# Loading q and k in 1 KB runs, with a fixed order of Pool and SP work, in a fused attention and mixer kernel

## The chip, the cores and the metric

The kernel runs on one core of a Trainium2 chip. The metric is the device time of one execution in microseconds (us). A run gives the median of several executions, and one execution is recorded by the hardware profiler. Executions of one kernel agree within 1.2% here (1.7% in e3, one of whose runs counts as slow). Comparisons use executions that ran on the same chip in the same rounds.

The engines are called PE (TensorE, matmuls), PEld (its weight loads), DVE or Vector, ACT or Scalar, POOL or Pool (GpSimd), and SP (SyncE, which here only issues transfers).

## The reference

There are 8 batches of 576 tokens with 8 heads of 64. Attention is limited to a window of 32 tokens on each side, plus 8 global tokens that see all and are seen by all. The result, 576 x 512 per batch, goes through a token mixer and a channel mixer:

```python
scores = scale * np.matmul(q, k.transpose(0, 1, 3, 2))       # q, k, v: (8, 8, 576, 64) float32
mask = (np.abs(pos[:, None] - pos[None, :]) <= 32) | is_global[:, None] | is_global[None, :]
attn = softmax(np.where(mask, scores, -1e9)); attn_out = np.matmul(attn, v)
x = attn_out.transpose(0, 2, 1, 3).reshape(8, 576, 512)
h = np.maximum(x^T @ w_tok1, 0.0) @ w_tok2;  u = x + h^T     # token mixer, 576 -> 256 -> 576
out = u + np.maximum(u @ w_ch1, 0.0) @ w_ch2                 # channel mixer, 512 -> 1536 -> 512
```

## The kernel before

The kernel is software-pipelined. While the channel mixer of batch b ("dense") keeps PE busy, the attention and token mixer of batch b+1 ("sparse") are threaded between its matmuls. Only batch 0 has nothing to hide behind, so the time has two parts: a **start**, up to the first channel matmul, and a **steady part**, from there to the end. A scheduler decides the order of the instructions on each engine when the kernel is built.

The parts that the change and the argument touch:

```python
# the list of global indices, to every partition: 8 low words out of 8 int64
nc.scalar.dma_start(out=gidx_b, in_=bass.AP(tensor=gt32, offset=0, ap=[[0, P], [2, NG]]))
# batch 0: q and k through SP in runs of 256 B (one token of one head)
    nc.sync.dma_start(out=n32[ti][:, 0 : NT - 1, h, :],
                      in_=ten[0, h, 0 : S - LAST, :].rearrange("(t p) d -> p t d", p=P))
# batches 1 to 7: Pool issues DMAs that cast float32 to float16 on the way
def load(b): ...
    nc.gpsimd.dma_start(out=dst[b % 2][0:n, t], in_=ten[b, :, P * t : P * t + n, :].rearrange("h p d -> p h d"))

def T(b, p):                                   # one pair of heads: ten transposes, two copies
    pT = pss([P, 2, 8 * P], F16, name=f"pT_{b}_{p}")
    for ti, n in enumerate((qn, kn)):
        for t in range(NT):                    # NT = 5, the last tile has 64 tokens and 64 rows of zeros
            nc.tensor.transpose(out=pT[:, ti, P * t : P * t + P], in_=n[b % 2][:, t, 2 * p : 2 * p + 2, :], identity=ident)
    nc.vector.tensor_copy(out=qTs[b % 2][:, p, :, GW:QS], in_=pT[:, 0, 0 : NT * P].rearrange("p (t x) -> p t x", t=NT))
    nc.vector.tensor_copy(out=kTs[b % 2][:, p, WIN:], in_=pT[:, 1, 0 : NT * P])

# S_(b, p): scores, exponentials on Scalar into e_all, then on Vector the product eg and for each head a mask:
        nc.vector.tensor_mul(out=eh, in0=eh, in1=bandm)            # 128 x 1040, float16
# PV(b, tau): values; the product with the global rows comes first, over 128 rows
            nc.tensor.matmul(ps[:, hf, 0 : NP * VW], lhsT=s["lf"][:, P * tau - sh : P * tau - sh + P],
                             rhs=s["rf"][:, 2 * hf : 2 * hf + 2], start=True, stop=False)
# M2: token mixer's second product, u = x + ...; M3: transposing DMA u -> uT; M4: first channel product from uT (b1p)
# gather(t): indirect DMAs that fetch the global rows of q and k (t = 0: batches 0-3, t = 1: batches 4-7)
```

The softmax here doesn't subtract the row's maximum and nothing guards it: scores larger than these inputs give would overflow.

Of the kernel before, what the change touches and what calls it, by code (L numbers as in the profile page):

```python
# [8 lines left out]
F32 = mybir.dt.float32  # L9
# [6 lines left out]
P = 128  # L16
# [26 lines left out]
def kernel(  # L43
# [30 lines left out]

    def pss(shape, dtype=F32, name="s"):
        return psS.tile(shape, dtype, tag="s", name=name)
# [8 lines left out]
    n32 = [mb.tile([P, NT, H, D], F32, tag="b1", bufs=1, name="n32_q")]  # L85
    n32 += [const.tile([P, NT, H, D], F32, name=f"n32_{n}") for n in "kv"]
# [15 lines left out]
    for ti, ten in enumerate((q, k)):  # L102
        nc.sync.dma_start(
            out=n32[ti][0:LAST, NT - 1], in_=ten[0, :, S - LAST : S, :].rearrange("h p d -> p h d")
        )
    for p in range(NP):
        for ti, ten in enumerate((q, k)):
            for h in (2 * p, 2 * p + 1):
                nc.sync.dma_start(
                    out=n32[ti][:, 0 : NT - 1, h, :],  # L110
                    in_=ten[0, h, 0 : S - LAST, :].rearrange("(t p) d -> p t d", p=P),
                )
    for c in range(NT):
        r0, r1, j0 = vrows(c)
        nc.sync.dma_start(
            out=n32[2][r0:r1, c], in_=v[0, :, j0 : j0 + (r1 - r0), :].rearrange("h p d -> p h d")
        )

    def load(b):
        for t in range(NT):  # L120
            n = P if t < NT - 1 else LAST
            for ten, dst in ((q, qn), (k, kn)):
                nc.gpsimd.dma_start(  # L123
                    out=dst[b % 2][0:n, t], in_=ten[b, :, P * t : P * t + n, :].rearrange("h p d -> p h d")
                )
        for c in range(NT):
            r0, r1, j0 = vrows(c)
            nc.gpsimd.dma_start(  # L128
                out=vsh[b % 2][r0:r1, c, :, 0:D],
                in_=v[b, :, j0 : j0 + (r1 - r0), :].rearrange("h p d -> p h d"),  # L130
            )

# [10 lines left out]
    make_identity(nc, ident)  # L143

# [30 lines left out]

    gather(0)


    for i in range(2):
        nc.vector.memset(qn[i][LAST:P, NT - 1], 0.0)  # L180
        nc.vector.memset(kn[i][LAST:P, NT - 1], 0.0)
        nc.vector.memset(vsh[i][0:WIN, 0], 0.0)
        nc.vector.memset(vsh[i][P - WIN : P, NT - 1], 0.0)
        nc.vector.memset(vsh[i][:, :, :, D + 1 : VW], 0.0)
        nc.vector.memset(vsh[i][:, :, :, D : D + 1], 1.0)
    e_all = const.tile([P, H, NT, EW], F16)
    nc.vector.memset(e_all[:, :, :, 0:64], 0.0)
    nc.vector.memset(e_all[:, :, 0, 64:P], 0.0)
    nc.vector.memset(e_all[:, :, NT - 1, 64 + GW + P :], 0.0)
    eg = const.tile([P, NT, H, GW], F16)  # L190
    qTs = [const.tile([P, NP, NT, QS], F16, name=f"qT{i}") for i in range(2)]
    kTs = [const.tile([P, NP, WIN + NT * P], F16, name=f"kT{i}") for i in range(2)]
    x16s = [const.tile([P, NT, DM], F16, name=f"x16_{i}") for i in range(2)]
    for i in range(2):
        nc.vector.memset(qTs[i][:, :, :, NG:GW], 0.0)
        nc.vector.memset(kTs[i][:, :, 0:WIN], 0.0)
    nc.vector.memset(kgz, 0.0)
    nc.vector.memset(x16s[0][LAST:P, NT - 1, :], 0.0)
    nc.vector.memset(x16s[1][0:LAST, NT - 1, :], 0.0)
# [7 lines left out]
    nc.vector.memset(w1l, 0.0)  # L207
    nc.vector.memset(w2[:, :, S:], 0.0)
# [3 lines left out]
    nc.gpsimd.dma_start(out=w2[:, :, 0:S], in_=moe_w_tok2.rearrange("(c p) x -> p c x", p=P))  # L212

# [11 lines left out]


    pm16 = int_op("pm16", 15, ALU.bitwise_and)
    p16 = int_op("p16", 4, ALU.logical_shift_right)
# [43 lines left out]

    band = const.tile([P, 192], F16)
    nc.gpsimd.memset(band, 1.0)
    left, right = band[:, 0:64], band[:, 64:192]
    nc.gpsimd.affine_select(out=left, in_=left, compare_op=ALU.is_ge, fill=0.0, base=0, pattern=[[1, 64]], channel_multiplier=-1)
    nc.gpsimd.affine_select(out=right, in_=right, compare_op=ALU.is_ge, fill=0.0, base=64, pattern=[[1, P]], channel_multiplier=-1)
    nc.gpsimd.affine_select(out=right, in_=right, compare_op=ALU.is_ge, fill=0.0, base=0, pattern=[[-1, P]], channel_multiplier=1)
# [14 lines left out]
    it_i = const.tile([P, NT * P], I32)  # L293
    nc.gpsimd.iota(it_i, pattern=[[1, NT * P]], base=0, channel_multiplier=0)
    mf = const.tile([P, NT * P], F16)
    it_f = const.tile([P, NT * P], F32)
# [5 lines left out]
    cc_i = const.tile([P, H], I32)  # L302
    nc.gpsimd.iota(cc_i, pattern=[[1, H]], base=0, channel_multiplier=0)
    blk = const.tile([P, H], F32)
    nc.vector.tensor_copy(out=blk, in_=cc_i)
    nc.vector.tensor_scalar(out=blk, in0=blk, scalar1=p16, scalar2=None, op0=ALU.is_equal)
# [16 lines left out]
    def cast0(p):  # L323

        for ti, dst in enumerate((qn, kn)):
            for t0, n, r in ((0, NT - 1, P), (NT - 1, 1, LAST)):
                hs = slice(2 * p, 2 * p + 2)
                (nc.scalar.copy if ti == 0 else nc.vector.tensor_copy)(  # L328
                    out=dst[0][0:r, t0 : t0 + n, hs], in_=n32[ti][0:r, t0 : t0 + n, hs]
                )  # L330
# [297 lines left out]
```

## Time and profile before

| before | value | from |
|---|---|---|
| time, median of 3 runs | 393.42 us (393.25 to 395.27) | runs |
| first scores | 44.6 us | timeline |
| first value product | 61.2 us | timeline |
| first channel matmul (end of the start) | 87.35 us | timeline |
| from there to the end of the span | 304.6 us | timeline |

The page gives the engines' busy time over the whole span:

```profile
PE 319.8 (82%) x2697; PEld 167.3 (43%) x2697; DVE 185.6 (47%) x400; ACT 137.2 (35%) x269; POOL 114.7 (29%) x156
```

That average mixes two regimes. In the steady part PE is the limit. The windows view (columns: window, its length, then busy us and instruction count of PE, PEld, DVE, ACT and POOL, the granted PE clock, DMA share, GB/s) shows a score stage of a later batch of the kernel before:

```profile
172.00:176.00 4.00, 4.00 (x40) 1.85 (x39) 3.15 (x8) 3.74 (x8) 1.68 (x2) 1.00 0.01 1
176.00:180.00 4.00, 3.71 (x49) 1.43 (x45) 3.05 (x7) 4.00 (x11) 4.00 (x6) 1.00 1.91 123
180.00:184.00 4.00, 4.00 (x42) 2.05 (x33) 3.00 (x6) 2.47 (x6) 3.73 (x6) 1.00 2.32 148
```

PE is full. But DVE stands at 3 us of every 4 there, and its results feed PE, so it has little room. (Pool is "busy" with issuing the casting DMAs, 873 ns each for q on the page.)

The places where PE waited in the steady part, from the waits view (total us, times, longest):

```profile
PE b1p_0_3083 L509 <- DMA uT_3004<-u_5_2972: 1.3, 1, 1.3
PE b1p_0_1117 L509 <- DMA uT_1038<-u_1_1006: 0.8, 1, 0.8
```

At the first channel matmul of each odd batch PE waits 0.7 to 2.0 us (0.79, 0.68, 1.30 and 2.00 in the timeline) for the transposing DMA (SP line 498), which turns u into uT.

Three groups of instructions of the page matter later (busy us, mean ns of one, idle time before and its releaser): the masks, the product eg, and the first scores.

```profile
L390 DVE TENSOR_TENSOR e_all<-e_all,bandm 128x1040 f16<-128x1040 f16 x64 | 42.4, 704 | 0.5
L384 DVE TENSOR_TENSOR eg<-e_all,bandm 128x160 f16<-128x160 f16 x32 | 7.7, 242 | 31.0 <-ACT e_all L383 31.0
L364 PE MATMUL s_0_0_288<-qT_168,kT_170 64*128 64x208 f16 x4 | 0.5, 357 | 14.5 <-POOL qT_168 L339 14.5
```

Finally the start. The DMA view of the first 16 us (first line: GB/s in 40 slices of 0.4 us; then a queue; then issues with KB each and median us to landing):

```profile
GB/s 0 0 0 0 0 0 5 61 152 111 0 0 0 0 0 0 0 0 0 0 0 0 0 0 0 0 0 0 0 0 0 12 38 52 76 94 109 156 176 214
q10 hardware_dynamic: 1184, 0.00, 3.3%
n_q<-in_q_dram SPq DMA_DIRECT2D x3, 128.0 KB, 16.0
gidx_b<-in_global_idx_dram ACTq DMA_DIRECT2D x1, 4.0 KB, 14.4
```

From 4 to 12.4 us the core moves next to nothing, with q and k already issued. A 4 KB index list takes 14.4 us to land.

### The profile page before, as it was taken

What the parts mean: (1) busy time and instruction counts of PE and PEld (TensorE: products, weight loads), DVE (VectorE), ACT (ScalarE), POOL (GpSimd) and SP (SyncE); (2) the same over time, 40 slices, a digit from 0 to 9 for tenths busy, and PEclk for the clock granted to TensorE, in tenths of its full rate; (3) what the DMA queues carried; (4) which work ended last, traced back from release to release, by engine and by line L of the source; (5) the groups of instructions that cost most, each with busy time, mean ns of one, the idle gap of its engine ahead of it and who ended that gap; (6) DMA issues with size and microseconds to landing.
All of it is one profiled execution on the core that took longest, in us unless ns stands there. A gap on an engine that the chain in (4) does not pass through costs nothing.

```text
span 391.9 us, 6622 instructions
## 1 busy us (share of the span) xinstructions
PE 319.8 (82%) x2697; PEld 167.3 (43%) x2697; DVE 185.6 (47%) x400; ACT 137.2 (35%) x269; POOL 114.7 (29%) x156
## 2 busy tenths in 40 slices
PE   0010255659999999999999999999899999997995
PEld 0010234324454465444544654455446545453552
DVE  5342254344645563566445635664456356644012
ACT  2001250106710861077118610761086107710610
POOL 4520798922820372028203720282000000000000
PEclk9999999688999999999999999999999999999999
DMA  0799999991985398419853984298600041005012
GB/s 14 122 198 206 182 141 94 122 114 8 125 79 147 21 115 75 136 30 129 79 147 22 117 75 135 35 126 81 145 0 2 28 136 28 2 28 149 0 55 80
DMA packets 143071, 34.56 MB, mean 88 GB/s; under 512 B 134336, under 2 KB 138304, under 8 KB 143040
## 3 DMA queue, kind: packets, MB, share of 16 engines
q0 software_dynamic: 102832, 16.42, 56.1%
q1 hardware_dynamic: 33776, 8.26, 11.2%
q10 hardware_dynamic: 6432, 9.44, 7.2%
q8 instruction: 21, 0.34, 0.4%
q14 instruction: 10, 0.08, 0.1%
HBM read 36.11 MB, written 9.44 MB: 116 GB/s over the span
## 4 chain that ended last, share of the span: by engine, by line
PE 59%; ACT 9%; DMA 3%; DVE 1%; SPq 1%; issue 1%; ACTq 0%
ACT e_all L374 2%; ACT e_all L383 2%; ACT e_all L382 1%; ACT e_all L381 1%; SPq L498 1%; DMA out_dram<-osb_0_2979 1%; DMA uT_3972<-u_7_3940 1%; PE op_4_4213 L535 1%; PE op_2_3013 L535 1%; PE op_2_2030 L535 1%; PE op_2_1047 L535 1%; PE op_2_3981 L535 1%; PE op_0_2938 L535 1%; PE op_0_3463 L535 1%; PE op_3_4197 L535 1%
## 5 line engine op out<-in xcount | busy, mean ns | idle before, releaser
L509 PEld LDWEIGHTS <-wc_184 128*128 128x128 f16 x384 | 33.0, 98 | 45.1 <-issue 15.8
L390 DVE TENSOR_TENSOR e_all<-e_all,bandm 128x1040 f16<-128x1040 f16 x64 | 42.4, 704 | 0.5
L123 POOL DMA_DIRECT2D qn_80<-in_q_dram x20 | 17.5, 873 | 60.6 <-PE pT_3_1738 L347 22.8
L439 PEld LDWEIGHTS <-e_all 128*128 128x128 f16 x320 | 25.2, 101 | 2.1 <-issue 1.0
L123 POOL DMA_DIRECT2D qn_79<-in_q_dram x15 | 13.2, 883 | 40.2 <-PE pT_3_1217 L347 20.1
L384 DVE TENSOR_TENSOR eg<-e_all,bandm 128x160 f16<-128x160 f16 x32 | 7.7, 242 | 31.0 <-ACT e_all L383 31.0
L128 POOL DMA_DIRECT2D vsh_84<-in_v_dram x20 | 16.9, 865 | 14.4 <-PE pv_2_916 L444 1.5
L347 PE MATMUL pT_0_266<-ident,qn_79 128*128 128x128 f16 x5 | 0.7, 309 | 23.1 <-ACT qn_79 L328 23.1
L444 PEld LDWEIGHTS <-e_all 128*128 128x128 f16 x256 | 19.0, 101 | 1.3
L347 PEld LDWEIGHTS <-qn_79 128*128 128x128 f16 x80 | 6.1, 106 | 28.4 <-ACT qn_79 L328 23.1
L364 PEld LDWEIGHTS <-kT_170 64*128 64x128 f16 x160 | 6.2, 103 | 27.4 <-issue 13.8
L123 POOL DMA_DIRECT2D kn_82<-in_k_dram x20 | 17.6, 878 | 0.0
L128 POOL DMA_DIRECT2D vsh_83<-in_v_dram x15 | 12.7, 881 | 9.6 <-PE b1lp_0_1385 L522 1.1
L328 ACT CAST qn_79<-n_q 64x128 f16<-64x128 f32 (+1 forms) x8 | 3.4, 456 | 32.8 <-DMA n_q<-in_q_dram 32.8
L481 PEld LDWEIGHTS <-w_183 128*128 128x128 f16 x80 | 8.2, 103 | 12.6 <-issue 4.8
L123 POOL DMA_DIRECT2D kn_81<-in_k_dram x15 | 13.3, 888 | 0.0
L364 PE MATMUL s_0_0_288<-qT_168,kT_170 64*128 64x208 f16 x4 | 0.5, 357 | 14.5 <-POOL qT_168 L339 14.5
L336 POOL CAST vsh_83<-n_v 32x512 f16<-32x512 f32 (+1 forms) x9 | 6.2, 697 | 19.3 <-DMA n_v<-in_v_dram 19.1
L522 PEld LDWEIGHTS <-wc_184 128*128 128x128 f16 x192 | 11.1, 98 | 0.6
L364 PEld LDWEIGHTS <-kT_171 64*128 64x128 f16 x160 | 5.2, 95 | 12.8 <-issue 8.5
L463 PEld LDWEIGHTS <-w_181 128*128 128x128 f16 x64 | 6.3, 101 | 6.4 <-issue 1.9
L539 DVE TENSOR_TENSOR osb_0_4162<-u_7_3940,op_0_4149 128x512 f32<-128x512 f16 x1 | 0.7, 689 | 17.1 <-PE op_0_4149 L535 17.1
(1059 smaller groups left out, 821.1 us busy)
## 6 DMA issues: line engine op xcount, KB each, us to landing
qn_80<-in_q_dram POOLq DMA_DIRECT2D x16, 128.0 KB, 4.6
kn_82<-in_k_dram POOLq DMA_DIRECT2D x16, 128.0 KB, 4.6
wc_184<-in_moe_w_ch_dram POOLq DMA_DIRECT2D x3, 512.0 KB, 10.3
wc_185<-in_moe_w_ch_dram POOLq DMA_DIRECT2D x3, 512.0 KB, 8.0
vsh_84<-in_v_dram POOLq DMA_DIRECT2D x12, 128.0 KB, 3.5
qn_79<-in_q_dram POOLq DMA_DIRECT2D x12, 128.0 KB, 4.2
kn_81<-in_k_dram POOLq DMA_DIRECT2D x12, 128.0 KB, 4.2
n_q<-in_q_dram SPq DMA_DIRECT2D x9, 128.0 KB, 7.6
```

The source lines that it names most:

```text
L123: nc.gpsimd.dma_start(out=dst[b % 2][0:n, t], in_=ten[b, :, P * t : P * t + n, :].rearrange("h p d -> p h d"))
L128: nc.gpsimd.dma_start(out=vsh[b % 2][r0:r1, c, :, 0:D], in_=v[b, :, j0 : j0 + (r1 - r0), :].rearrange("h p d -> p h d"),)
L364: nc.tensor.matmul(ps[:, par, off : off + n], lhsT=kT[r, P * c : P * c + P], rhs=qf[r, lo : lo + n], start=True, stop=True,)
L374: nc.scalar.activation(out=e2[:, :, 1:3, 64:EW], in_=s1[:, :, 0 : 2 * W].rearrange("p h (c x) -> p h c x", c=2), func=AF.Exp, scale=scale)
L383: nc.scalar.activation(out=e2[:, :, 3, 64:EW], in_=s2[:, :, 2 * QS : 2 * QS + W], func=AF.Exp, scale=scale)
L390: nc.vector.tensor_mul(out=eh, in0=eh, in1=bandm)
L439: nc.tensor.matmul(o, lhsT=e_all[:, h, tau, EW - P - sh : EW - sh], rhs=vsh[b % 2][:, tau, h, :], start=False, stop=last and tau == NT - 1,)
L444: nc.tensor.matmul(o, lhsT=e_all[:, h, tau + 1, 0:P], rhs=vsh[b % 2][:, tau + 1, h, :], start=False, stop=last)
L481: nc.tensor.matmul(ps[:, i, :], lhsT=w2[:, ch, P * tau - sh : P * tau - sh + P], rhs=s["a1"][:, ch, :], start=(ch == 0), stop=(ch == 1),)
L509: nc.tensor.matmul(ps, lhsT=wc1[:, cc, P * j : P * j + P], rhs=s["uT"][:, cc, :], start=(cc == 0), stop=(cc == 3))
L522: nc.tensor.matmul(ps[:, i, :], lhsT=wc1[:, cc, P * j : P * j + P], rhs=s["uTl"][:, cc, :], start=(cc == 0), stop=(cc == 3),)
L535: nc.tensor.matmul(ps, lhsT=w, rhs=wc2[:, j, :], start=(j == 0), stop=(j == NJ - 1))
```

## The change

The intent was to load q and k in runs of 1 KB. Four neighbouring tokens of a head lie together in memory, so each partition takes four tokens in place of one. The transposes then leave the tokens of a tile interleaved in PSUM, and the copies out of PSUM, with a step of 128 elements, put them in order. All loads go through SP in float32 with casts on Pool; the order of Pool and SP instructions is fixed to program order; the large weights are issued behind the v casts. Three more edits ride along: tail transposes of only 64 rows, a global-row product of 64 rows in two halves, and the first batch's u transposed on PE.

```diff
+    ctx.enter_context(tc.manual_schedule(engines={mybir.EngineType.Pool, mybir.EngineType.SP}))
+    def load_qk(b, hs):
+        for ten, dst in ((q, lq), (k, lk)):
+            nc.sync.dma_start(out=dst[:, hs].rearrange("p h i d -> p h (i d)"),
+                in_=ten[b, hs, 0 : S - LAST, :].rearrange("h (p i) d -> p h (i d)", i=4))
 ... (the same for the tail and for v; memsets moved from Vector to Pool, e_all's behind the gather and the weights)
+    def cast(b):                                                   # on Pool, batches 1 to 7
+        for src, rest, dst in ((lq, lqr, qn[b % 2]), (lk, lkr, kn[b % 2])):
+            nc.gpsimd.tensor_copy(out=dst[:, 0:4].rearrange("p i h d -> p h i d"), in_=src)
+            nc.gpsimd.tensor_copy(out=dst[0:LAST, NT - 1], in_=rest)
 ...
     def T(b, p): ...
+                r = P if t < NT - 1 else LAST                      # 64-row transposes of the tail
-                    out=pT[:, ti, P * t : P * t + P], in_=n[b % 2][:, t, ...], identity=ident
+                    out=pT[:, ti, P * t : P * t + r], in_=n[b % 2][0:r, t, ...], identity=ident[0:r, 0:r]
-        nc.vector.tensor_copy(out=qTs[b % 2][:, p, :, GW:QS], in_=pT[:, 0, 0 : NT * P]...)
-        nc.vector.tensor_copy(out=kTs[b % 2][:, p, WIN:], in_=pT[:, 1, 0 : NT * P])
+        pm = pT[:, :, 0:512].rearrange("p n (i t x) -> p n t x i", i=4, t=4)
+        nc.vector.tensor_copy(out=qT[:, 0:4, GW:QS].rearrange("p t (x i) -> p t x i", i=4), in_=pm[:, 0])
+        nc.vector.tensor_copy(out=qT[:, 4, GW : GW + LAST], in_=pT[:, 0, 512:S])
+        nc.vector.tensor_copy(out=kT[:, WIN : WIN + 512].rearrange("p (x i) -> p x i", i=4),
+            in_=pT[:, 1, 0:512].rearrange("p (i x) -> p x i", i=4))
+        nc.vector.tensor_copy(out=kT[:, WIN + 512 : WIN + S], in_=pT[:, 1, 512:S])
 ...
+            r = slice(64 * hf, 64 * hf + 64)                       # PV: the global-row product in two halves
-                ps[:, hf, 0 : NP * VW], lhsT=s["lf"][:, ...], rhs=s["rf"][:, 2 * hf : 2 * hf + 2], ...
+                ps[:, hf, 0 : NP * VW], lhsT=s["lf"][r, ...], rhs=s["rf"][r], ...
 ... (batch 0: transposes on PE in place of the transposing DMA; loop: cast, globals, castv, then the loads of b + 2)
```

## The prediction

> **What bounds the kernel now.** Two regimes. From 100 us on TensorE decides: the windows view gives PE 38.3 to 39.7 us busy of every 40, and one batch takes about 39 us (token-mixing evictions at 115.2 and 193.5 us are two batches apart). Before that PE is mostly idle, 40 us busy in 100. The timeline shows why: the first full q slice is cast at 22.4 us, because 256 B runs of q and k share the DMA with the weights (windows 20 to 40: 197 to 207 GB/s). The first scores start at 44.56 us; the waits list 14.5 us for the Pool copy of the global columns into qT, which stands on Pool behind a v cast that waited 19.1 us for v. Value products start at 61.2, the first channel matmul at 87.35 us after 2.8 us of waiting for the transposing DMA.
>
> **At the start (all on the critical path).**
> 1. q and k come in 1 KB runs. From the page's queue table, engine time per packet is about 21 ns at 245 B (queue 1) and 70 ns at 1467 B (queue 10). I estimate 54 ns for 1 KB: 2.1 MB in 7 us, all q/k landed by 13 us instead of 40.
> 2. The large weights wait for the v casts. I put them at 36 to 60 us, early enough.
> 3. The global copy stands before the v casts. What now limits the scores is the chain index list (14.4 us to land before; estimate 8 to 12), indices, four gathers (1.3 us apart), about 3 us of weight issues and about 7 us of memsets now on Pool (estimate from 195 ns for 128 and 272 ns for 192 elements). First scores at about 29 us, 15.5 us earlier.
> 4. From scores to values runs a latency chain of 3.85 us a pair; slower qT/kT copies add about 0.6 us a pair: 2 us lost.
> 5. Batch 0's transposing DMA becomes PE transposes: 2 to 3 us gained.
> Net about 16 us gained.
>
> **In the steady state.**
> - qT/kT copies read PSUM in steps of 128 elements. [...] now 640 elements take 0.48 us. Estimate 0.65 us each plus two 0.15 us tails: +2.2 us DVE a batch, at 75% DVE load in the score stage.
> - Pool casts about 12 us a batch (128x512 cast: 0.61 us) in place of 13 us of DMA issue. [...] a mask pair took 1.73 us beside Pool casts, 1.30 alone. About +1 us DVE a batch.
> - The global-row product becomes two 64-row matmuls side by side (64-row score matmuls, four of 208 columns in 0.35 us, already overlap): -0.11 us x 5 a batch; narrower tail transposes -0.2.
> PE gains 0.75 us a batch and loses about as much to DVE stalls. Net near 0 (-5 to +10 in all).
>
> **Predicted: 376 us**, 8 in 10 between 362 and 387. Faster by over 2%: 0.85; within 2%: 0.12; slower: 0.03.
>
> **What would show it.** First scores near 29 us, released by Pool; first channel matmul near 71 us; from there to the end 303 to 306 us (304.5 now); qT/kT copies of 512 near 0.65 us; a pair of global-row matmuls in one's time; HBM bytes unchanged.
>
> **What would make it wrong.** Index list or Pool memsets 5 us off either way; large weights late at the first channel matmul; DVE and Pool contention stalling PE in each score stage (2 us a batch would cost 14); PE gains without stalls (down to 365).

At the start the sum is 15.5 us gained, 2 lost and 2 to 3 gained, so about 16; in the steady part it is near 0; 393.4 less 16 is about 377, put down as 376. The 0.65 us of a strided copy and the 0.15 us of a tail stand as estimates, beside the 0.48 us that the trace shows for 640 contiguous elements; so do the -0.11 and -0.2 us for PE. The +1 us from Pool casts rests on one sighting in the trace of before (1.73 us for a pair of masks, against 1.30).

## The result, and the profile after

| | before | after |
|---|---|---|
| median of the common runs | 394.35 us (393.25 to 395.98, 4 runs) | 432.06 us (430.1 to 432.58, 4 runs) |
| first scores | 44.6 | 34.9 |
| first value product | 61.2 | 67.3 |
| first channel matmul | 87.35 | 88.76 |
| from there to the end | 304.6 | 341.4 |
| mean distance of batches 1 to 6 | 39.7 | 45.7 |

The ratio is 1.094, with a 95% interval from 1.089 to 1.100. A ratio here is the mean time of one kernel's fast runs over that of the other's of the same rounds, so it is not quite the ratio of the quoted medians. The predicted 376 us, with a range to 387, was wrong in direction. Neither half came out: the 16 us at the start are missing, and the steady part, predicted level, costs 37 us more.

The page's busy times after:

```profile
PE 338.9 (79%) x2713; PEld 165.4 (38%) x2713; DVE 224.7 (52%) x443; ACT 137.5 (32%) x269; POOL 122.4 (28%) x165
```

And the groups of the page that answer to those shown of before. The Pool cast at L343 is new.

```profile
L405 DVE TENSOR_TENSOR e_all<-e_all,bandm 128x1040 f16<-128x1040 f16 x64 | 55.7, 910 | 0.5
L399 DVE TENSOR_TENSOR eg<-e_all,bandm 128x160 f16<-128x160 f16 x32 | 16.2, 505 | 3.8 <-ACT e_all L398 3.8
L343 POOL CAST qn_84<-lq 128x2048 f16<-128x2048 f32 x4 | 7.6, 1890 | 111.3 <-DMA lq<-in_q_dram 59.0
```

DVE is busy 39 us longer. Of that, 22 us are the same masks and eg products, untouched in the code, which now take 910 ns in place of 704 and 505 in place of 242. PE is busy 19 us longer although its work was meant to shrink.

The windows of a score stage after:

```profile
180.00:184.00 4.00, 3.15 (x21) 1.11 (x20) 4.00 (x6) 3.17 (x7) 2.86 (x2) 1.00 1.16 324
184.00:188.00 4.00, 3.52 (x29) 1.68 (x29) 2.93 (x6) 2.19 (x5) 3.12 (x4) 1.00 0.93 195
...
192.00:196.00 4.00, 2.32 (x27) 0.98 (x25) 3.91 (x6) 2.08 (x5) 3.91 (x5) 1.00 0.00 0
```

DVE has reached 4 of 4 us and PE has fallen to 2.3 to 3.5: the limit has moved. The timeline of the same stretch shows why (start, us busy; in brackets the idle time before it and what ended it):

```profile
180.72 3.00 DVE L405 TENSOR_TENSOR e_all<-e_all,bandm 128x1040 f16<-128x1040 f16 x2
181.14 2.03 POOL L343 CAST qn_83<-lq 128x2048 f16<-128x2048 f32 x1 [32.44 <-PE s_3_1_1770 L379]
183.65 0.68 DVE L364 COPY kT_124<-pT_2_1749 128x512 f16<-128x512 f16 x1
184.48 0.52 PE L356 MATMUL pT_3_1795<-ident,qn_84 128*128 128x128 f16 x5 [1.33 <-DVE kT_124 L368]
184.93 0.53 PE L356 MATMUL pT_3_1795<-ident,kn_86 128*128 128x128 f16 x5
```

A pair of masks took 3.00 us beside a Pool cast of q. In batch 1, with no Pool work beside it, a pair took 1.31 us (100.98 us of the same trace); the four entries of the next batch took 1.60 to 2.12. The k copy stood behind that pair, and PE waited 1.33 us for the copy.

Why do the two meet? The bracket of the Pool cast names a score matmul, but that matmul doesn't touch the buffer qn, and such a bracket only names what came last by the profile. The data came then: SP issued this load of q at 173.22 us, right behind the transposing DMAs of the batch before, and the trace has it landed at 180.99, 0.15 us before the cast. The next cast of q shows it openly:

```profile
173.22 0.64 SPq L107 DMA_DIRECT2D lq<-in_q_dram  x1
225.15 1.89 POOL L343 CAST qn_84<-lq 128x2048 f16<-128x2048 f32 x1 [29.07 <-DMA lq<-in_q_dram]
```

All five casts of q from batch 3 on start 0.14 to 0.15 us after their q has landed. So the collision is built in, by the arrival of the data: SP holds the loads behind the transposing DMAs at the end of a batch, and 6 to 8 us later, when q lands, Vector is in the score stage.

The waits of PE, the largest in the steady part after:

```profile
PE b1p_0_3181 L537 <- DMA uT_3093<-u_5_3061: 3.0, 1, 3.0
PE b1p_0_2168 L537 <- DMA uT_2080<-u_3_2048: 2.7, 1, 2.7
PE b1p_0_1155 L537 <- DMA uT_1067<-u_1_1035: 2.6, 1, 2.6
PE pv_0_2385 L447 <- DVE rf_2377 L432: 1.4, 1, 1.4
PE pT_3_1795 L356 <- DVE kT_124 L368: 1.3, 1, 1.3
```

The waits for the transposing DMA have grown to about 3 us, and many new ones end with DVE. The wait has a second cost. First the timeline at the first channel matmul of batch 3 after, then the windows of 2 us there (the granted clock is the third number from the end):

```profile
218.50 1.86 PE L537 MATMUL b1p_0_2168<-uT_2080,wc_168 128*128 128x512 f16 x4 [2.66 <-DMA uT_2080<-u_3_2048]
```

```profile
218.00:220.00 2.00, 1.50 (x4) 0.59 (x5) 0.00 (x0) 0.00 (x0) 0.00 (x0) 0.51 0.41 93
220.00:222.00 2.00, 2.00 (x10) 0.79 (x8) 0.00 (x0) 0.72 (x2) 0.00 (x0) 0.64 0.81 218
```

Such a boundary in the timeline of the kernel before (to batch 1):

```profile
125.11 1.02 PE L509 MATMUL b1p_0_1117<-uT_1038,wc_184 128*128 128x512 f16 x4 [0.79 <-DMA uT_1038<-u_1_1006]
126.83 0.44 PE L347 MATMUL pT_1_1129<-ident,qn_79 128*128 128x128 f16 x5
127.11 0.44 PE L347 MATMUL pT_1_1129<-ident,kn_81 128*128 128x128 f16 x5
```

After a wait of 2.66 us the granted clock is about half, and four channel matmuls take 1.86 us in place of 1.02. The last two lines show one more thing: five transposes of q and the next five of k start 0.28 us apart before (126.83, 127.11), and 0.45 us apart after (184.48, 184.93, shown above). Over the whole trace the median is 279 ns before and 452 ns after. The groups with a narrow transpose are slower.

At the start, two waits of DVE are telling:

```profile
15.46 0.17 DVE L235 CAST gidx_f<-gidx_b 128x8 f32<-128x8 int32 x1 [11.46 <-DMA gidx_b<-in_global_idx_dram]
64.41 0.23 DVE L313 CAST g_q_150<-g_q_146 128x128 f16<-128x128 f32 x1 [11.44 <-DMA g_q_146<-in_q_dram,idx_i]
```

The index list comes at 15.5 us. And Vector, which ran its instructions in the order of the build, stood 11.44 us on the *second* gather, whose rows are for batches 4 to 7, while batch 0's values waited behind it.

The first scores of after were released by Pool:

```profile
34.89 0.53 PE L379 MATMUL s_0_0_281<-qT_121,kT_123 64*128 64x208 f16 x4 [3.25 <-POOL qT_121 L347]
```

That copy of the global columns ends a chain which starts with the list: Vector turns the list into indices, Pool issues the gathers from 19.33 us on and then works without a pause until the copy at 34.19. The first q had been transposed long before, at 17.76.

### The profile page after: what moved, and what is told of

It reads as the page before. It is cut to its first block, busy times and chain, and to the rows that moved or that the text cites. A ratio compares the mean times of both kernels' runs of the same rounds, so it can differ in the third digit from the quotient of the medians.

```text
span 430.1 us, 6780 instructions
## 1 busy us (share of the span) xinstructions
PE 338.9 (79%) x2713; PEld 165.4 (38%) x2713; DVE 224.7 (52%) x443; ACT 137.5 (32%) x269; POOL 122.4 (28%) x165
## 3 DMA queue, kind: packets, MB, share of 16 engines
q10 hardware_dynamic: 6432, 9.44, 6.3%
HBM read 36.11 MB, written 9.44 MB: 106 GB/s over the span
## 4 chain that ended last, share of the span: by engine, by line
PE 55%; DVE 21%; DMA 10%; POOL 6%; ACT 3%; SPq 2%; issue 2%; POOLq 0%; DVEq 0%; ACTq 0%
DVE e_all L405 9%; DMA lk<-in_k_dram 3%; DMA g_q_146<-in_q_dram,idx_i 3%; DVE eg L399 3%; SPq L526 2%; POOL vsh_87 L339 1%; DVE qT_121 L362 1%; DVE kT_123 L364 1%; DVE x_0_181 L468 1%; DMA uT_2080<-u_3_2048 1%; DMA uT_4097<-u_7_4065 1%; DMA uT_1067<-u_1_1035 1%; DVE qT_122 L362 1%; DMA uT_3093<-u_5_3061 1%; PE a1p_585 L480 1%
## 5 line engine op out<-in xcount | busy, mean ns | idle before, releaser
L405 DVE TENSOR_TENSOR e_all<-e_all,bandm 128x1040 f16<-128x1040 f16 x64 | 55.7, 910 | 0.5
L537 PEld LDWEIGHTS <-wc_168 128*128 128x128 f16 x384 | 32.5, 101 | 52.1 <-issue 19.9
L343 POOL CAST qn_84<-lq 128x2048 f16<-128x2048 f32 x4 | 7.6, 1890 | 111.3 <-DMA lq<-in_q_dram 59.0
L343 POOL CAST qn_83<-lq 128x2048 f16<-128x2048 f32 x3 | 5.8, 1937 | 62.4 <-PE s_3_1_1770 L379 32.4
L456 PEld LDWEIGHTS <-e_all 128*128 128x128 f16 x320 | 20.2, 101 | 5.5 <-issue 1.1
L339 POOL CAST vsh_88<-lv 32x512 f16<-32x512 f32 x24 | 19.8, 825 | 7.2 <-DMA g_k_148<-in_k_dram,idx_i 6.4
L339 POOL CAST vsh_87<-lv 32x512 f16<-32x512 f32 x24 | 18.5, 770 | 1.0
L461 PEld LDWEIGHTS <-e_all 128*128 128x128 f16 x256 | 18.1, 102 | 0.0
L399 DVE TENSOR_TENSOR eg<-e_all,bandm 128x160 f16<-128x160 f16 x32 | 16.2, 505 | 3.8 <-ACT e_all L398 3.8
L356 PEld LDWEIGHTS <-qn_83 128*128 128x128 f16 (+1 forms) x80 | 7.2, 108 | 26.8 <-ACT qn_83 L329 17.8
L498 PEld LDWEIGHTS <-w_167 128*128 128x128 f16 x80 | 7.8, 98 | 11.0 <-issue 2.5
L567 DVE TENSOR_TENSOR osb_0_4287<-u_7_4065,op_0_4274 128x512 f32<-128x512 f16 x1 | 0.7, 686 | 21.4 <-PE op_0_4274 L563 21.4
L550 PEld LDWEIGHTS <-wc_168 128*128 128x128 f16 x192 | 11.2, 98 | 0.9
L427 PEld LDWEIGHTS <-eg 128*32 128x32 f16 x160 | 3.2, 99 | 17.2 <-DVE eg L399 12.8
L482 ACT ACTIVATE a_0_596<-a1p_585 128x1024 f16<-128x1024 f32 x1 | 1.0, 1024 | 25.7 <-PE a1p_585 L480 25.7
L480 PEld LDWEIGHTS <-w_165 128*128 128x128 f16 x64 | 6.5, 102 | 6.7 <-issue 1.9
L356 PEld LDWEIGHTS <-qn_84 128*128 128x128 f16 (+1 forms) x80 | 6.0, 96 | 8.0 <-issue 3.5
L343 POOL CAST kn_86<-lk 128x2048 f16<-128x2048 f32 x4 | 7.8, 1957 | 3.9 <-DMA lk<-in_k_dram 3.9
L336 POOL CAST vsh_88<-lv 128x512 f16<-128x512 f32 x12 | 8.7, 758 | 0.3
```

What stands on the lines that cost most here:

```text
L336: nc.gpsimd.tensor_copy(out=vsh[b % 2][:, c, :, 0:D], in_=lv[:, c])
L339: nc.gpsimd.tensor_copy(out=vsh[b % 2][a : a + 32, c, :, 0:D], in_=lv[a : a + 32, c])
L343: nc.gpsimd.tensor_copy(out=dst[:, 0:4].rearrange("p i h d -> p h i d"), in_=src)
L356: nc.tensor.transpose(out=pT[:, ti, P * t : P * t + r], in_=n[b % 2][0:r, t, 2 * p : 2 * p + 2, :], identity=ident[0:r, 0:r])
L399: nc.vector.tensor_tensor(out=eg[:, :, 2 * p : 2 * p + 2, :], in0=e2[:, :, :, P:QS].rearrange("p h c x -> p c h x"), in1=bandm[:, :, 64:80 ...
L456: nc.tensor.matmul(o, lhsT=e_all[:, h, tau, EW - P - sh : EW - sh], rhs=vsh[b % 2][:, tau, h, :], start=False, stop=last and tau == NT - 1,)
```

## The experiments

The theory after reading the traces had four causes for the steady loss: (N) the narrow tail transposes, (S) the strided copies, (C) Pool casts colliding with two-input Vector work, (H) the halved global-row product. For the start it was the second gather standing in Vector's order, and later the index list. The rivals were one dominant cause, usually C, or a general contention with the transfers. Each steady figure below is the distance in time between the first channel matmuls of batch 0 and batch 7 in the profiled run: 273.6 us before and 307.7 after, so there are 34.1 us to explain. All profiled runs were fast except that of e3.

### e1: the second gather issued earlier

```diff
@@ in the start's loop / after the loads of batch 1
+            gather(1)        # right after the first copy of the global columns
-    gather(1)
```

> After, with only the second gather of global rows moved on Pool: right behind the first copy of the global columns instead of behind the v casts, the large weight issues and the pads. Theory S (the 11.4 us that Vector stood before the cast of the gathered rows at 64.4 us is the lost start gain, since Vector's order is fixed and the last mask of batch 0 stands behind that cast): that wait falls under 2 us, the first channel matmul comes at 78 to 80 us instead of 88.8, the time is 420 to 424 us. Rival (the large weights bound the first channel matmul anyhow): it stays near 88 and the time stays near 432. Both leave the mean interval between the first channel matmuls of batches 1 to 6 at 45.7 us (39.7 before).

Measured: 427.64 us, ratio 1.0835 (1.0774 to 1.0895) against 1.0944 of the changed kernel. First channel matmul 86.99, steady 308.0. The gather's wait did not go; it moved to an earlier point and halved:

```profile
41.30 0.23 DVE L313 CAST g_q<-g_q 128x128 f16<-128x128 f32 x1 [5.78 <-DMA g_q<-in_q_dram,idx_i]
```

The channel matmul was expected at 78 to 80 us, so the theory was met only in part: an earlier issue does not take the wait away, because its reader on Vector moved forward with it.

### f5: the second gather read late

The gather and its reader move into the loop of batch 1; nothing needs the rows before batch 4.

```diff
-    gather(1)
-    gather_t(1)
+        if b == 1:
+            gather(1)
+            gather_t(1)
```

> After, with the second gather of global rows and the casts, transposes and copies that use it moved behind the dense work of batch 0 (they serve batches 4 to 7). Theory S: nothing of batch 0 stands behind that gather any more on Vector, so the 11.4 us wait goes and is not replaced (in the run that moved only the gather, a wait of 5.8 us came in its place): value products at 56 to 58 us instead of 67.3, first channel matmul at 77 to 80, time 420 to 423. Rival (the weights or something else bounds the first channel matmul): it stays at 86 or later.

Measured: 426.03 us, ratio 1.0802 (1.0758 to 1.0846). First value product at 61.2 in place of 67.3, first channel matmul at 84.0 in place of 88.76. Steady 309.1, 1.4 us more than after. The second gather cost the start 6.1 us up to the first values and 4.8 us up to the channel matmul, less than the 9 to 12 expected.

### e2: batches 1 to 7 by casting DMA, no Pool casts

```diff
+            src = ten[b, :, 0 : S - LAST, :].rearrange("h (p i) d -> i p h d", i=4)
+            for i in range(4):
+                nc.gpsimd.dma_start(out=dst[:, i], in_=src[i])     # float32 -> float16 on the way, same token order
 ...
-            cast(b + 1); castv(b + 1); load_rest(b + 2); load_qk(b + 2, slice(0, H)); load_v(b + 2)
+            load_sw(b + 2)
```

> After, but batches 1 to 7 come by casting DMA from Pool (as before), still in the permuted token order, so no casts on Pool and the strided PSUM copies stay. Theory C (Pool casts run beside Vector's masks in the score stage and stretch both): mask of 1040 back from 910 to about 700 ns, intervals of batches 1 to 6 shrink from 45.7 to about 41 us, time about 408 us. Rival D (the four strided copies are the load on Vector): intervals stay at 44 to 46 us, time over 423.

Measured: 411.29 us, ratio 1.0428 (1.0381 to 1.0476). Steady 291.6. The masks are back:

```profile
L418 DVE TENSOR_TENSOR e_all<-e_all,bandm 128x1040 f16<-128x1040 f16 x64 | 42.6, 707 | 0.5
```

So 16.1 of the 34.1 us belong to the Pool casts and all that hangs on them, and 18.0 do not: C alone is not the answer.

### e3: the same Pool casts, moved to the value stage

A copy of one element on Pool ties the casts to the first value product of the batch in work, when the masks are done. The amount of casting is the same.

```diff
+    def casts(b):
+        nc.gpsimd.tensor_copy(out=gt, in_=x16s[(b - 1) % 2][0:1, 0, 0:1])
+        cast(b); globals_(b); castv(b)
-        u += [(0.8, lambda t=t: PV(b, t)) for t in range(NT)]
+        u += [(0.8, lambda: PV(b, 0))] + [(0.0, lambda: casts(b + 1))] + [(0.8, lambda t=t: PV(b, t)) for t in range(1, NT)]
```

> After, with the same casts on Pool, but tied by one tiny Pool copy to the first value product of the batch in work, so that they run in the value and token-mixing stage and not in the score stage. Theory C in its narrow form (it is the collision with the two-input masks, not the Pool work): mask back to about 710 ns, intervals about 41 us, time about 408. If the collision costs the same wherever it falls: intervals 44 to 46, time near 430. Rival D: the same as no effect.

Measured: 418.04 us, 417.11 for the three fast runs alone, whose ratio is 1.0575 (1.0502 to 1.0647); the profiled run was slow (a span of 419.1 us), so its figures are rough. Steady 293.5, and the masks are whole again with 80.7 us of Pool casts still in the trace:

```profile
L405 DVE TENSOR_TENSOR e_all<-e_all,bandm 128x1040 f16<-128x1040 f16 x64 | 43.1, 714 | 0.5
```

This separates the collision from the casts: what costs is *when* they run, beside the masks, not that they exist. The traces settle the rival, a general contention with the transfers, too. In the trace of after, 21 of the 64 masks had no Pool cast, copy or memset beside them and took 696 ns in the mean, 702 at most; the 32 that ran beside such work for 90% of their time or more took 1,064. In e3, 23 masks ran without Pool work while the DMA moved over 150 GB/s, and they took 701 ns in the mean. (The start came 4.4 us later, first channel matmul at 93.16, with the casts of batch 1 standing elsewhere; that is most of why the total is worse than e2's.)

### e4: batches 1 to 7 in natural token order

256 B runs, two contiguous copies a pair, 128-row tail transposes; the Pool casts stay.

```diff
+    def load_nat(b):
+            for t in range(4):
+                nc.sync.dma_start(out=dst[:, :, t], in_=ten[b, :, P * t : P * t + P, :].rearrange("h p d -> p h d"))
-                r = P if t < NT - 1 else LAST
+                r = P if t < NT - 1 or b > 0 else LAST
+        if b > 0:
+            nc.vector.tensor_copy(out=qT[:, :, GW:QS], in_=pT[:, 0, 0 : NT * P].rearrange("p (t x) -> p t x", t=NT))
+            nc.vector.tensor_copy(out=kT[:, WIN:], in_=pT[:, 1, 0 : NT * P])
```

> After, but batches 1 to 7 keep the token order of before (256 B runs) and so two contiguous PSUM copies in place of four; casts stay on Pool. The scheduler then also puts TensorE's order back: 36 matmuls instead of 30 between the last eviction of u and the next channel matmul of odd batches. Theory C alone: mask stays at about 900 ns, intervals at 44 us or more. Rival D with theory O (the strided copies load Vector, and through the scheduler they take 1.3 us of cover from the transposing DMA): that wait falls from 2.6 to 3.4 us to about 1 us, intervals fall to about 42 us, time about 410.

Measured: 411.17 us, ratio 1.0407 (1.0338 to 1.0476). Steady 289.5: 18.2 us of the loss go with S and N together. The waits for uT at the odd batches fall to 0.43 to 0.95 us, but the masks stay slow (810 ns) and PE still waits for Vector in the score stage. The 15.9 us left over the kernel before are put down to C and H, which this run does not separate.

### f2: the kernel before, with only the tail transposes narrowed

```diff
+                r = P if t < NT - 1 else LAST
+                    out=pT[:, ti, P * t : P * t + r], in_=n[b % 2][0:r, t, 2 * p : 2 * p + 2, :], identity=ident[0:r, 0:r]
 ... (two memsets, and the copies cut to 576 tokens, q's in two pieces: a third copy a pair on Vector)
```

> The kernel before with one part of the change alone: the last token tile is transposed from 64 rows to 64 columns, not 128 (the copies then take 576 of the 640 columns). Theory M [...]: a group of five transposes takes 0.45 us from its start to the next group, not 0.28, as seen in the kernel after; 8 groups a batch cost 1.4 us, the time rises by 8 to 12 us to 402 to 406. Rival, as predicted: narrower is cheaper by 0.2 us a batch, the time falls by 1 to 2 us.

Measured: 410.64 us, ratio 1.0407 (1.037 to 1.0445). An edit that halves two of ten transposes costs 17 us, more than the 8 to 12 expected. In the profiled runs, 12.5 of that are between batches 0 and 7, 3.7 in the start and 1.5 behind. The five transposes of q and of k in this run:

```profile
209.02 0.52 PE L350 MATMUL pT<-ident,qn 128*128 128x128 f16 x5
209.47 0.53 PE L350 MATMUL pT<-ident,kn 128*128 128x128 f16 x5
```

They start 0.45 us apart (median 452 ns over the trace), against 279 ns before. There are eight such groups a batch and seven batches in the steady distance: 8 x 0.173 x 7 = 9.7 us. Waits at the odd boundaries, 7.3 us against 4.8, make up most of the rest; how much of these comes from the third copy is not separated. What the traces show is the loss: a group that goes from four 128-row transposes to one of 64 rows and back takes 0.17 us longer. In the trace of after (the group at 184.48) the 128-row transposes start 55 ns apart, the 64-row one 152 ns after the fourth, and the next 128-row one 132 ns after that.

### f3: the kernel before, with only the global-row product halved

```diff
-                ps[:, hf, 0 : NP * VW], lhsT=s["lf"][:, ...], rhs=s["rf"][:, 2 * hf : 2 * hf + 2], start=True, stop=False,
+                ps[:, hf, 0 : NP * VW], lhsT=s["lf"][64 * hf : 64 * hf + 64, ...], rhs=s["rf"][64 * hf : 64 * hf + 64], start=True, stop=False,
```

> The kernel before with one part of the change alone: the product of the global rows as two 64-row matmuls side by side in place of two of 128 rows. As predicted: 0.11 us less a value tile, 40 tiles, so 4 us less (389.5). Theory M: the two overlap, but the change of row mode before and after them takes back what they win, so the time stays within 1 us of before and a value tile keeps its 0.72 us from its first matmul to the next tile's work.

Measured over 5 rounds: 395.32 us, ratio 1.0029 (1.0002 to 1.0056); steady 276.4 against 273.6. The predicted gain of 0.11 x 5 us a batch, 4 us in all, is absent, and the sign is rather the other. In the kernel after, the two halves do start together (6 ns apart, 0.29 us for both):

```profile
196.00 0.29 PE L447 MATMUL pv_0_1902<-rf_1894,lf_1869 64*128 64x264 f16 x2 [1.34 <-DVE rf_1894 L432]
196.22 0.20 PE L456 MATMUL pv_0_1902<-vsh_88,e_all 128*128 128x66 f16 x1
...
196.72 0.59 PE L537 MATMUL b1p_11_2008<-uT_1601,wc_168 128*128 128x512 f16 x2
```

But the next 128-row matmul follows only 0.22 us later, so a value tile takes 0.72 us from first matmul to the next tile's work (196.00 to 196.72). Before it took the same 0.72 us (69.90 to 70.62), in which the next matmul followed each of the two 128-row products by 0.12 us (69.90 to 70.02, 70.26 to 70.38). Two times 0.12 against 0.22: the halves saved next to nothing.

### f4: the kernel before, with only the permuted order and four copies

```diff
+                if t < NT - 1:
+                    src = ten[b, :, 0 : S - LAST, :].rearrange("h (p i) d -> i p h d", i=4)[t]
+                nc.gpsimd.dma_start(out=dst[b % 2][0:n, t], in_=src)
 ... (for b > 0 the four copies of the change, with 128-row tails)
```

> The kernel before with one part of the change alone: the permuted token order for batches 1 to 7 (casting DMA as before, 128-row tail transposes as before) and so four copies out of PSUM, two of them in steps of 128 elements. Theory O (the longer Vector chain makes the scheduler place 30 instead of 36 matmuls before the first channel matmul of odd batches; the wait for the transposing DMA grows by about 2 us there, and after a wait that long the granted TensorE clock falls to about half for some 4 us): waits of 2.5 to 3.5 us at the four odd batches, granted clock under 0.8 right after them, time up by 10 to 16 us (404 to 410). Rival (the copies are hidden, as DMA and Vector have room): within 2 us of before.

Measured: 406.73 us, ratio 1.0307 (1.0269 to 1.0346). First channel matmul 86.75, steady 286.2: the copies, with the permuted casting DMAs that they need, cost 12.5 us, against about 0 predicted net. In the steady part PE waited for little but uT (five waits, the first of which belongs to the start):

```profile
PE b1p L521 <- DMA uT<-u: 16.1, 5, 4.3
```

At the four odd boundaries these waits are 2.93, 2.86, 3.28 and 4.27 us where before has 0.79, 0.68, 1.30 and 2.00: 8.6 us more. The granted clock fell after all four, to 0.50 or 0.51 in the second 2 us behind the first channel matmul. The time that the clock's fall took, (1 - clock) x 2 us summed over the windows of the 10 us behind the first channel matmul of batches 0 to 6, is 6.8 us here and 1.7 before. Waits and clock together, 8.6 + 5.1, slightly over-explain the 12.5.

Why the waits grow by more than the copies' own time was only read, not tested. In the built order of PE's instructions, 36 matmuls stand between the second u product of an odd batch, whose u the transposing DMA reads last, and its first channel matmul in the kernel before. In the changed kernel and in f4 there are 30, in e4 36 again. So the scheduler placed the u products later against the dense work, and there is less to cover the transposing DMA with. The traces allow an estimate. The wait at an odd boundary grew by 2.1 us in the mean. Six matmuls less, at 0.22 us each (18 of 512 columns take 4.05 us in f2's trace), are 1.3 of that. The other 0.85 lies behind Vector: from the end of the second u to the first channel matmul before takes 5.7 us in the mean and f4 6.55, so the stretch in which the transposing DMA stands took longer. No run forced one order on both kernels, so this part stays a reading.

### g1 and g2: the index list as one run

By now one thing of the start was open: in both kernels nothing but the list moves between 4 and 12 us. The edit fetches the 64 bytes of the list whole for each partition, and takes the low words on the chip:

```diff
-    gidx_b = const.tile([P, NG], I32)
-    nc.scalar.dma_start(out=gidx_b, in_=bass.AP(tensor=gt32, offset=0, ap=[[0, P], [2, NG]]))
+    gidx_b = const.tile([P, NG, 2], I32)
+    nc.scalar.dma_start(out=gidx_b.rearrange("p g w -> p (g w)"), in_=bass.AP(tensor=gt32, offset=0, ap=[[0, P], [1, 2 * NG]]))
-    nc.vector.tensor_copy(out=gidx_f, in_=gidx_b)
+    nc.vector.tensor_copy(out=gidx_f, in_=gidx_b[:, :, 0])
```

On the kernel before:

> The kernel before with one thing changed: the list of global indices is loaded to every partition as one run of 64 bytes in place of eight elements of 4 bytes. Theory A (the list's 1024 four-byte packets hold up the transfers of q and k: in both kernels, from 4 to 12 us, the trace has hardly anything else moving): q and k start some 8 us sooner, so the first scores fall from about 44.6 to about 36 us and the time from 394 to about 386 (384 to 390). Theory B (q and k start late for another reason, such as the start of the queue): the list comes sooner, but q, k and the time stay (within 2 us of 394), since before's scores did not wait for the list. Distance from first channel matmul to the end 304 to 306 under both.

On the changed kernel:

> The changed kernel with the same edit of the index list. Theory A: list and q/k arrive some 8 to 10 us sooner; the gathers are issued sooner; first scores from 34.9 to about 26 us, first channel matmul from 88.8 to about 80, time from 432 to about 424 (421 to 427). Theory B: the list alone comes sooner; the first scores wait for q and k instead and gain at most 4 us, and the second gather's wait (11.4 us on Vector) takes part of that back: time 428 to 432. The steady distance from the first channel matmul to the end stays at 341 to 344 us under both.

Measured: g1 387.68 us, ratio 0.9823 (0.9777 to 0.9869); first scores 37.2, first channel matmul 79.52, steady 274.6. g2 422.9 us, ratio 1.0719 (1.0672 to 1.0767); first scores 25.8, first channel matmul 78.9, steady 308.5. Theory A holds in both: in g2 the first transposes of q start at 8.69 us in place of 17.76. The first scores alone would not tell this in the changed kernel, since there they wait for the chain that the list itself starts; its gathers were issued from 10.24 us on in place of 19.33. The windows of the kernel before, from 4 to 12 us, and then those of g1 (the last two numbers are DMA share and GB/s):

```profile
4.00:8.00 4.00, 0.00 (x0) 0.00 (x0) 2.97 (x15) 0.90 (x4) 0.35 (x1) 1.00 0.05 0
8.00:12.00 4.00, 0.00 (x0) 0.00 (x0) 2.27 (x14) 0.00 (x0) 2.88 (x3) 1.00 0.04 0
```

```profile
4.00:8.00 4.00, 0.00 (x0) 0.00 (x0) 2.97 (x15) 0.90 (x4) 0.35 (x1) 1.00 0.68 89
8.00:12.00 4.00, 0.00 (x0) 0.00 (x0) 3.76 (x27) 0.00 (x0) 2.88 (x3) 1.00 1.24 239
```

In the second window the DMA share went from 0.04 to 1.24 with no other edit. The list, 1,024 pieces of 4 bytes in 14.4 us, had held up q and k for some 8 us. The packets on that queue in the first 16 us were 1,184 before, and 288 with the edit. So this list, issued by Scalar, held back loads that SP had issued.

### g3 and g4: a version from the findings

g3 keeps of the change what helped the start and undoes what cost the steady part. Batch 0 is loaded in 1 KB runs and transposed on PE. Batches 1 to 7 come by casting DMA in natural order with two contiguous copies. Tails and the global-row product have 128 rows again. The second gather is read in the loop of batch 1, the list comes as one run, e_all is cleared before the gather, and the small weights are issued behind the v casts. Pool and SP keep their fixed order.

```diff
-            cast(b + 1); castv(b + 1); load_rest(b + 2); load_qk(b + 2, slice(0, H)); load_v(b + 2)
+            load_sw(b + 2)                                        # casting DMA, natural order
+        if b > 0:
+            nc.vector.tensor_copy(out=qT[:, :, GW:QS], in_=pT[:, 0, 0 : NT * P].rearrange("p (t x) -> p t x", t=NT))
+            nc.vector.tensor_copy(out=kT[:, WIN:], in_=pT[:, 1, 0 : NT * P])
+            return
 ... (r = P for all tails; the 128-row product; gather(1), gather_t(1) at b == 1; the list of g1)
```

> A version put together from the findings: the changed kernel's 1 KB loads and PE transposes for batch 0 alone; batches 1 to 7 by casting DMA in natural token order with two contiguous copies a pair; 128-row tail transposes; the 128-row global-row product; the second gather read in batch 1's loop; the index list as one run; the memsets of e_all ahead of the gather; small weights behind the v casts. If the three steady causes (narrow tail transposes, strided copies, Pool casts beside masks) are the whole loss, the distance from first channel matmul to end returns to before's 304 to 306 us, with the mask near 704 ns and the mean interval of batches near 39.1 us. The start: first scores at 18 to 22 us, first channel matmul at 62 to 70. Time 368 to 375. If something else in the fixed Pool and SP order costs steady time, the distance stays over 310 us and the time over 378.

Measured: 374.69 us, ratio 0.948 (0.9437 to 0.9523). First scores 21.1, first channel matmul 65.53, steady 275.3, within 2 us of before. The masks of g3 on its page, and PE's waits in its steady part:

```profile
L415 DVE TENSOR_TENSOR e_all<-e_all,bandm 128x1040 f16<-128x1040 f16 x64 | 42.6, 707 | 0.5
```

```profile
PE b1p L545 <- DMA uT<-u: 3.9, 3, 1.9
PE hp L506 <- DVE u L511: 2.3, 1, 2.3
```

This is the check on the list of causes: with N, S, C and H undone, and with the fixed order of Pool and SP still there, the loss of 34 us is gone but for 1.6. The fixed order alone is thus not a cause. But g3 has no loads on SP in the steady part, so it does not test that order together with the loads, which set when the casts ran.

g4 is g3 with the two strided q copies of each pair of batch 0 on Scalar in place of Vector:

```diff
-        nc.vector.tensor_copy(out=qT[:, 0:4, GW:QS].rearrange("p t (x i) -> p t x i", i=4), in_=pm[:, 0])
-        nc.vector.tensor_copy(out=qT[:, 4, GW : GW + LAST], in_=pT[:, 0, 512:S])
+        nc.scalar.copy(out=qT[:, 0:4, GW:QS].rearrange("p t (x i) -> p t x i", i=4), in_=pm[:, 0])
+        nc.scalar.copy(out=qT[:, 4, GW : GW + LAST], in_=pT[:, 0, 512:S])
```

> The version before it with the two strided q copies of each pair of batch 0 on the Scalar engine in place of Vector. If Vector's row (q copy, masks, k copy) sets the pace of batch 0's pairs, each of four pairs comes about 0.7 us sooner and the time falls by 1 to 4 us against the version before it; if Scalar's exponentials or latency set it, the time is the same or up to 2 us worse. Steady distance unchanged.

Measured: 371.09 us, ratio 0.9409 (0.9364 to 0.9455), 3.6 us less than g3 in the same rounds. First channel matmul 61.44, steady 275.4. The pairs of batch 0 come 4.73 us apart in place of 5.59 (the last two intervals). So Vector set their pace. This version beats both kernels: 5.9% less than before, 14% less than after (371.09 against 432.06, medians of different rounds).

### The steady loss added up

| steady distance, batch 0 to 7 | us | against before |
|---|---|---|
| before | 273.6 | |
| before + narrow tails (f2) | 286.1 | +12.5 |
| before + strided copies (f4) | 286.2 | +12.5 |
| before + halved product (f3) | 276.4 | +2.8 |
| after without narrow tails and strided copies (e4) | 289.5 | +15.9 |
| after without Pool casts (e2) | 291.6 | +18.0 |
| after with the Pool casts moved (e3, slow profiled run) | 293.5 | +19.9 |
| after | 307.7 | +34.1 |
| all undone (g3) | 275.3 | +1.6 |

N and S cost 25.0 us one by one, but only 18.2 us come off when both leave the changed kernel (34.1 - 15.9). Both lengthen the same waits for uT, so they do not add fully.

The other way to add it up is by what PE did in the trace of after against before. Waits for uT are 11.7 us against 4.8 (+6.9). The other waits of PE over the same distance (those over 0.15 us), nearly all for Vector in the score stages and just ahead of the value products, are 14.7 against 0.8 (+13.9). Slower transposes give 9.7 by the reckoning of f2. The lower clock behind the boundaries, counted as for f4, is 4.9 against 1.7 (+3.2). Together that is 33.7 of 34.1 us, an estimate, since the four parts are not measured apart.

## Why the prediction was wrong

It erred in both halves. At the start its sum was 15.5 us gained up to the first scores, 2 lost from there to the values, and 2 to 3 gained by the PE transposes. Measured were 9.7 gained, 15.8 lost and 4.7 gained, so 1.4 lost in all. The step that failed most is thus "from scores to values". In the steady part the step that failed is "Net near 0": two edits that were counted as a gain or as hidden (narrower transposes, strided copies) each cost 12.5 us alone, and the Pool casts 16. Point by point:

- **"q and k come in 1 KB runs ... all q/k landed by 13 us instead of 40."** The time of a packet was right: the 2,048 packets of 1 KB took 57 ns in the mean (52 in the median), 54 estimated. What failed is the arrival: they moved between 12.9 and 22.2 us, most of them from 15 to 20. The diagnosis behind it failed too: the prediction put the late first slice of q down to 256 B runs beside the weights, but with the list alone mended (g1), still in 256 B runs, that slice was cast at 12.43 us in place of 22.40. The runs were held up behind the index list, which g1 and g2 show: taking its small pieces away moved the first transposes of q in the changed kernel from 17.76 to 8.69 us. The prediction used the list's 14.4 us as a private delay of the indices, and guessed that it would shrink to 8 to 12; it had no reason to, and it took about 13.9 (issued at 1.53, used from 15.46).
- **"First scores at about 29 us."** They came at 34.9, released by Pool as predicted. The chain was right, and its first term, the list, was mis-sized: with the list mended the first scores came at 25.8. (In the kernel before, they moved from 44.6 to 37.2.)
- **"From scores to values ... 2 us lost."** Measured: 32.5 us from first scores to first values, against 16.7 before, so 15.8 us lost. This is the term that ate the start's gain. About 6 us are the second gather in Vector's order (f5), which the prediction did not mention. About 6.5 are the pairs themselves, 6.40, 5.82 and 5.82 us apart in place of 3.85. In the timeline the k copy stands behind both masks on Vector; I had estimated 0.6 us a pair from the copy's own length, and left out where it stands. (g4 shows that Vector sets this pace; no run moved the k copy.) The remaining 3 us or so are not separated by a run.
- **"The large weights wait for the v casts ... early enough."** Right: no wait for weights shows ahead of the first channel matmul.
- **"Batch 0's transposing DMA becomes PE transposes: 2 to 3 us gained."** Right in sign. From first values to first channel matmul after took 21.4 us, before 26.1, and the wait of 2.76 us for the transposing DMA is gone; no run separates the PE transposes from the rest of the change.
- **"qT/kT copies ... 0.65 us each plus two 0.15 us tails."** Right in size: 685 ns (the mean of q's and k's) and 180. In the traces 512 elements with a step of 128 took 685 ns where 640 contiguous ones took 485. What failed is the step from there to "net near 0". At the odd boundaries PE's work had just about covered the chain from Vector through u and uT (waits of 0.7 to 2.0 us), and what was added came out as PE idle time and a lower clock (f4: 12.5 us), by f4's estimate through the order of PE's instructions and a longer stretch from u to the first channel matmul (6.55 us in place of 5.7).
- **"About +1 us DVE a batch" from Pool casts.** The collision was named, and rightly; the size was off. Masks took 206 ns more each and eg 263 ns: 64 x 0.206 + 32 x 0.263 = 21.6 us in all, 2.7 a batch, on an engine with little room (e2, e3: 14 to 16 us of time). The prediction scaled one sighting, 1.73 us for a pair, and did not ask when the casts would run. They are released when their data land, 6 to 8 us after SP has issued the loads of q at the end of a batch, and so in the score stage of the next. The largest sighting in the trace of after: 3.00 us for a pair in place of 1.31. Why Vector slows beside them no run shows.
- **"The global-row product ... -0.11 us x 5 a batch."** Wrong: 0.72 us a tile either way, and no gain in the time (f3).
- **"Narrower tail transposes -0.2."** Wrong in sign: f2 cost 12.5 us in the steady part. The prediction counted rows and columns of the matmul and left out what a 64-row transpose costs in the middle of a run of 128-row ones, 0.17 us a group of five.
- **"From there to the end 303 to 306 us."** 341.4.
- **"HBM bytes unchanged."** Right: 36.11 MB read and 9.44 written in both.

The line "DVE and Pool contention stalling PE in each score stage (2 us a batch would cost 14)" in the prediction's own list of risks is what happened, but it was given almost no weight: 0.03 for slower.

What stays open: why the stretch from u to the first channel matmul took longer in f4, and a test of the order of PE's instructions; the last 3 us between scores and values; and the sign of the halved product, where 2.8 us in one trace stand against 0.3% in the time.

## What to carry to other kernels

Before changing the size of transfers, look at a window of the DMA view in which nothing moves and ask which transfer was in flight. Here one list of 4-byte elements cost the start 7.8 us (before) and 9.9 us (after) up to the first channel matmul, and one small edit mended it. An edit that saves work on an engine may be paid for elsewhere on it (64-row transposes between 128-row ones: 452 ns a group of five in place of 279) or in order (a copy behind two masks), so measure each small edit alone before bundling it. And for work that is moved to a "free" engine, ask what releases it and when: here the casts ran as soon as their data landed, and the loads had been issued at such a time that they landed in Vector's busiest stage. Beside two-input Vector work Pool casts were in the wrong place (a mask of 696 ns took 1,064); the same casts tied to a later stage (e3) did no harm to the masks.

## What these runs show of the hardware

- A list of small elements issued by one engine held back another's loads: 1,024 pieces of 4 bytes, issued by Scalar, took 14.4 us, and from 4 to 12 us the loads that SP had issued moved nothing, at a DMA share of 0.04 to 0.05. With the list as one 64-byte run a partition the share was 0.68 and 1.24.
- A 64-row transpose among 128-row ones made a group of five take 452 ns in place of 279. Two 64-row halves (two 264-column products started together) gained nothing: 0.72 us a tile either way.
- Pool casts beside two-input Vector work stretched it: a pair of 128 x 1040 masks took 3.00 us beside Pool casts (one of 128 x 2048, 2.03 us, and the start of a small one), and 1.31 alone; the mean mask went from 704 to 910 ns.
- The granted PE clock fell behind the longer waits for uT at a first channel matmul. In before, after and f4, ten such waits took 2.58 us or more (one of 2.76 in before; 2.58, 2.66, 3.04 and 3.41 in after; five that come to 16.1 in f4, 4.27 the longest), and in the 4 us behind each the clock was at 0.50 or 0.51 in at least one window of 2 us. The waits of 0.68, 0.79, 1.30 and 2.00 us in before were followed by 1.00. The length alone may not decide: in e2, whose waits for uT come to 9.1 us, the clock stayed at 1.00 behind two of the four odd boundaries (126.4 and 378.8 us).
